# Four experts' results turned by VectorE and carried to rows by transfers, in a fused LSH attention and expert layer

## The chip, the cores and the metric

The kernel runs on one core of one Trainium2 chip. The metric is device time in microseconds (us) of one execution. The core has five engines that matter here: TensorE (PE, with its weight loads shown apart as PEld), VectorE (DVE), ScalarE (ACT), GpSimd (POOL) and SyncE (SP), which here only issues transfers. Each engine takes its own instructions in order and waits for the others by semaphores. SBUF is the core's working memory with 128 partitions, PSUM the memory that TensorE writes.

## The reference

Attention over 4 batches and 8 heads, 768 positions of 64 numbers, where a query sees only the keys in its own hash bucket; then a layer of 8 experts in which each of the 3072 tokens goes to the one expert with the highest gate:

```python
q_bucket = np.sum((np.einsum('bhsd,dk->bhsk', q, proj) > 0) * powers, axis=-1)   # same for k
scores = np.where(q_bucket[..., None] == k_bucket[..., None, :], scale * q @ k.T, -1e9)
x = (softmax(scores) @ v).transpose(0, 2, 1, 3).reshape(3072, 512)
expert_idx = np.argmax(x @ w_gate, axis=1)
gate_w = softmax(x @ w_gate)[np.arange(N), expert_idx]
for e in range(8):                          # tokens sorted by expert
    h = np.maximum(x_sorted[lo:hi] @ w1[e], 0.0)      # 512 -> 1024
    y_sorted[lo:hi] = h @ w2[e]                       # 1024 -> 512
return gate_w[:, None] * y_sorted[inv_perm]
```

The change concerns the expert layer alone.

## The kernel before

**Stages.** The attention part runs first (to about 435 us). Its result rows, with gate and token number behind them, are scattered to a DRAM table `xs`, one region for each expert. Then come the experts in phases `n` of the loop at the end of the kernel function. The experts are ranked by their number of tokens (the first one is picked early). Rank 0 has two phases, n = 0 and 1, of 256 tokens each; n = 2 to 8 are ranks 1 to 7. `PH[n]` holds rank, offset and capacity, from `CAPS`. Tokens beyond a capacity go to a spill loop at the end.

**A phase.** `mm1(n, f)`, f = 0 to 7, makes the 1024 hidden features in eight products of 128 features. Each float32 operand is held as a high and a low part, and three of the four part products are summed, so one result takes 12 matmuls in the first half and 24 in the second. ScalarE writes the ReLU's high part (L827), VectorE the low part (L829). `mm2(n, m)`, m = 0 to 3, makes the output. For the four wide ranks 1 to 4 the output comes feature by token: ScalarE copies it to `YT` (L851), and in the next phase `yout(n - 1, f // 2)` stands behind every second `mm1`: four matmuls with the identity (L876) turn 128 tokens back to rows, VectorE multiplies with the gate (L878), and GpSimd sends the rows to the output by an indirect transfer (L880). For the others (`by_token`) the second product is computed token by feature at once (L867, and in halves at the very end L900).

**Widths.** `products` (L769) runs the first matmul of a group over the whole capacity, and the others over one of four widths in `WIDTHS`, picked by branches from the expert's real length.

**Tokens of the next phase.** `rows(n + 1)`, at a phase's start, loads the next tokens with SP in four transfers (L712) and their gates and numbers in one (L714). `blocks` turns them from SBUF to SBUF by VectorE in 32x32 blocks (L736), and `xt` makes the high part by a ScalarE copy (L755) and the low part by a VectorE subtraction (L756), a quarter of the features at a time. The tables `WHEN` and, for n = 1, `SOON` say behind or within which `mm2` each quarter stands.

**Weights.** They come in chunks, four to an expert: two of w1 and two of w2. SP loads each chunk in halves of 512 KB (`raw_load`, L680) into four buffers; `halves` has ScalarE write the high part (L693) and GpSimd the low part (L694), a quarter of a chunk behind each `mm1` and two behind each `mm2`. Six chunks fit. In SP's order a phase starts with the rows, then the load of the second half of the next expert's second chunk follows (called at f = 1), and its conversion stands at f = 6.

The order of every engine's instructions is the order of the program text.

Of the kernel before, what the change touches and what calls it, by code (L numbers as in the profile page):

```python
# [21 lines left out]
DM = H * D  # L22
# [12 lines left out]
FLOOR = -float(2 ** 33)  # L35
LOW = -float(2 ** 100)

WIDTHS = [(), (456, 440, 432, 416), (432, 424, 408, 392), (408, 400, 388, 372), (396, 384, 376, 360),
          (384, 368, 356, 344), (372, 356, 348, 340), (354, 344, 336, 324)]


EARLY = 256
CAPS = [512, 456, 432, 408, 396, 384, 372, 354]
ROW = N + 128
FILL = 512
NONE = 1 << 20
# [7 lines left out]


@with_exitstack
def lsh_attention_moe(ctx, tc, qk2, v, proj, wg, w1, w1q, w2, out):
    nc = tc.nc
    const = ctx.enter_context(tc.tile_pool(name="const", bufs=1))
    moe = ctx.enter_context(tc.tile_pool(name="moe", bufs=1))  # L60
# [604 lines left out]
    def raw_load(c, a):  # L665

        r, k = divmod(c, 4)
        if k < 2:
            w = w1q if r else w1
            src = w[bass.ds(EV[r], 1)].rearrange("o (a p) f -> p (o a) f", p=128)[:, 2 * a:2 * a + 2,  # L670
                                                                               k * 512:(k + 1) * 512]
        else:
            o = (k - 2) * 4 + 2 * a
            src = w2[bass.ds(EV[r], 1)].rearrange("o (a p) d -> p (o a) d", p=128)[:, o:o + 2, :]
        n = 2 * c + a
        if n < 10 or n % 2:
            t = moe.tile([128, 2, 512], F32, name="raw", bufs=2)
        else:
            t = P2["p"].tile([128, 2, 512], F32, name="raw2", bufs=2)
        nc.sync.dma_start(t, src)  # L680
        RAW[c, a] = t
# [46 lines left out]

        return x[:, d * PW + E:d * PW + E + 2 * D]

    def blocks(n, j):

        if j == 0:
            XT[n] = P2["p"].tile([128, 4, 512], F32, name="xt")
        if j < len(tiles_of(PH[n][2])):
            nc.vector.transpose(XT[n][:, :, 128 * j:128 * j + 128].rearrange("p c (t i) -> p t c i", i=32),  # L736
                                XG[n][:, 4 * j:4 * j + 4].rearrange("p t w -> p (t w)"))

    def xt(n, d):
        r, o, c = PH[n]  # L740
        if d == 0:
            XH[n] = (moe.tile([128, 2, 4, EARLY], F32R, name="xhe") if n < 2 else
                     P2["p"].tile([128, 2, 4, CAPS[1]], F32R, name="xh"))
        t = len(tiles_of(c))
        if n > 1:
            p = XT[n][:, d]
        else:
            p = ps.tile([128, 512], F32, name="t", bufs=2)
            for j in range(t):
                nc.tensor.transpose(p[:, j * 128:(j + 1) * 128], heads(XG[n][:, j], d), ident)  # L750
        if d == 0:
            GT[n] = moe.tile([128, 4], F32, name="gate", bufs=3)
            nc.vector.tensor_copy(GT[n][:, :t], XI[n][:, :t, 0] if n > 1 else XG[n][:, :t, GC])
            tokens(n)
        nc.scalar.activation(XH[n][:, 0, d, :c], p[:, :c], AF.Copy)  # L755
        nc.vector.tensor_tensor(XH[n][:, 1, d, :c], p[:, :c], XH[n][:, 0, d, :c], op=OP.subtract)  # L756
# [72 lines left out]
            nc.vector.scalar_tensor_tensor(h1[:, f, :c], p[:, :c], 0.0, h0[:, f, :c], op0=OP.max, op1=OP.subtract)  # L829

    def by_token(n):
        return PH[n][2] <= 384

    def mm2(n, m, mid=None):

        r, o, c = PH[n]
        if by_token(n):
            yout(n, m, mid)
            return
        if m == 0:  # L840
            YT[n] = (wk.tile([128, 4, EARLY], F32, name="qk") if n == 0 else
                     P2["p"].tile([128, 4, CAPS[1]], F32, name="yt"))
        h = HH[n]
        ms = slice(m * 128, (m + 1) * 128)
        p = ps.tile([128, 512], F32, name="s", bufs=3)
        if mid:
            mid()

        terms = [(CH[4 * r + 2 + f // 4][:, a, f % 4, ms], h[b][:, f]) for f in range(8) for a, b in ((0, 0), (0, 1), (1, 0))]
        products(n, p, c, terms)  # L850
        nc.scalar.activation(YT[n][:, m, :c], p[:, :c], AF.Copy)  # L851

    def yout(n, j, mid=None):
        r, o, c = PH[n]
        if j >= len(tiles_of(c)):
            return
        i, pw = tiles_of(c)[j]
        if n + 1 == len(PH) and j + 1 == len(tiles_of(c)):
            youts(n, j, i, pw)
            return  # L860
        p = ps.tile([128, 512], F32, name="s", bufs=3)
        if by_token(n):
            k = 0
            for f in range(8):
                w = CH[4 * r + 2 + f // 4]
                for a, b in ((0, 0), (1, 0), (0, 1)):
                    nc.tensor.matmul(p[:pw], HH[n][b][:, f, i:i + pw], w[:, a, f % 4],  # L867
                                     start=(k == 0), stop=(k == 23))
                    k += 1
                    if k == (12 if n else 20) and mid:  # L870
                        mid()
        else:

            yw = max(pw, min(128, CAPS[1] - i))
            for m in range(4):
                nc.tensor.transpose(p[:yw, m * 128:(m + 1) * 128], YT[n][:, m, i:i + yw], ident)  # L876
        y = (P2["p"] if n else moe).tile([128, DM], F32, name="y" if n else "ye", bufs=3 if n else 2)
        nc.vector.tensor_scalar(y[:pw], p[:pw], GT[n][:pw, j:j + 1], None, op0=OP.mult)  # L878
        nc.gpsimd.memset(C["spacer"], 0.0)
        st = nc.gpsimd.indirect_dma_start(out=out, out_offset=bass.IndirectOffsetOnAxis(ap=IX[n][:pw, j:j + 1], axis=0),  # L880
                                          in_=y[:pw], in_offset=None, bounds_check=N - 1, oob_is_err=False)
        for q in outs:
            tc.declare_no_dep(st.ins, q.ins, reason="rows of other tokens")
        outs.append(st)

    def youts(n, j, i, pw):

        r = PH[n][0]
        y = P2["p"].tile([128, DM], F32, name="y", bufs=3)
        ix = P2["p"].tile([128, 2], I32, name="ix2")  # L890
        for s in range(2):
            nc.vector.tensor_scalar(ix[:, s:s + 1], IX[n][:, j:j + 1], 2.0, float(s), op0=OP.mult, op1=OP.add)
        for s in range(2):
            cs = slice(s * DM // 2, (s + 1) * DM // 2)
            p = ps.tile([128, 512], F32, name="s", bufs=3)
            k = 0
            for f in range(8):
                w = CH[4 * r + 2 + f // 4]
                for a, b in ((0, 0), (1, 0), (0, 1)):
                    nc.tensor.matmul(p[:pw, :DM // 2], HH[n][b][:, f, i:i + pw], w[:, a, f % 4, cs],  # L900
                                     start=(k == 0), stop=(k == 23))
                    k += 1
            nc.vector.tensor_scalar(y[:pw, cs], p[:pw, :DM // 2], GT[n][:pw, j:j + 1], None, op0=OP.mult)
            st = nc.gpsimd.indirect_dma_start(out=out.rearrange("n (s d) -> (n s) d", s=2),
                                              out_offset=bass.IndirectOffsetOnAxis(ap=ix[:pw, s:s + 1], axis=0),
                                              in_=y[:pw, cs], in_offset=None, bounds_check=2 * N - 1, oob_is_err=False)
            for q in outs:
                tc.declare_no_dep(st.ins, q.ins, reason="other parts of the rows")
            outs.append(st)
# [241 lines left out]


    WHEN = (((), (0,)), ((1,), (2,)), ((3,), ()), ((), ()))
    SOON = (((), ()), ((0, 1), (2, 3)), ((), ()), ((), ()))
    raw_load(5, 0)
    plan = spill_plan()
    for n in range(1, len(PH)):
        c0 = 4 * (PH[n][0] + 1)
        last = n + 1 == len(PH)
        if not last:  # L1160
            rows(n + 1)
            length(n + 1)
        for f in range(8):
            mm1(n, f)
            if f % 2 and not by_token(n - 1):
                yout(n - 1, f // 2)
            halves(c0, f)
            if 3 <= n < 6:
                for _ in range(2):
                    next(plan, None)  # L1170
        for m in range(4):
            mid, end = ((), ()) if last else (WHEN if n > 1 else SOON)[m]
            if m == 0 and not last:
                for j in range(4):
                    blocks(n + 1, j)
            if not (last and m == 3):
                mm2(n, m, lambda: xts(n + 1, mid))
            halves(c0 + 2, 2 * m)
            halves(c0 + 2, 2 * m + 1)
            xts(n + 1, end)  # L1180
        if n == 6:
            for _ in plan:
                pass
        if n == 7:
            C["n"] = nc.values_load(C["cntn"][0:1, 0:1], min_val=0, max_val=TMAX)
# [65 lines left out]
```

## Time and profile before

| | |
|---|---|
| median of 3 runs | 717.42 us (715.97 to 718.87) |
| profiled execution | 715.64 us, span 713.8 us |
| TensorE busy, weight loads busy | 691.8 us, 560.5 us |
| VectorE, ScalarE, GpSimd busy | 491.0, 410.9, 487.6 us |
| DMA, mean over the span | 194 GB/s |
| mean granted TensorE clock | 0.994 of full speed |

The times come from runs without a profile, the rest from one profiled execution. Matmuls are pipelined and their ends are modelled, so a busy TensorE may still be waiting; weight loads are told by their own starts. A page row gives the busy time of a group of instructions, the mean of one, and behind the bar the idle time of the engine before them with what ended it.

### The profile page before, as it was taken

To read this page: it belongs to the slowest core of one execution; us is meant where nothing else is said; L and a number is where in the kernel's file an instruction comes from. 1 tells how busy PE (TensorE), PEld (TensorE's weight loads), DVE (VectorE), ACT (ScalarE), POOL (GpSimd) and SP (SyncE) were. 2 spreads that over 40 slices of the span, in tenths; PEclk is the share of its full clock that TensorE was granted. 3 is DMA by queue.
4 is the path that set the end of the run, shared out by engine and by line. 5 is a ranking of instruction groups with operands and counts; after the bars stand their busy time and mean duration, and the time that the engine had idled before them with its cause. 6 is when DMAs were issued, how large, how long until landed. Compare 5 with 4: busy or idle time off the path is not lost.

```text
span 713.8 us, 13651 instructions
## 1 busy us (share of the span) xinstructions
PE 691.8 (97%) x4539; PEld 560.5 (79%) x4539; DVE 491.0 (69%) x942; ACT 410.9 (58%) x830; POOL 487.6 (68%) x729
## 2 busy tenths in 40 slices
PE   8889999999999999999998999999999999999996
PEld 4677668667766776676666788899999999989895
DVE  7998898889888988898998673424676825232321
ACT  5786678668766876787676633544444444444310
POOL 7766676678777777877785663686666667768522
PEclk8999999999999999999999999999999999999999
DMA  8888779868867677687678247683847474747201
GB/s 324 277 232 234 252 229 289 230 183 233 246 198 213 198 202 226 212 258 185 201 206 234 90 143 217 204 216 120 200 127 199 139 194 139 195 161 202 93 12 40
DMA packets 67775, 138.33 MB, mean 194 GB/s; under 512 B 12883, under 2 KB 29523, under 8 KB 67680
## 3 DMA queue, kind: packets, MB, share of 16 engines
q1 hardware_dynamic: 60848, 120.67, 59.4%
q0 software_dynamic: 6688, 16.35, 6.8%
q8 instruction: 61, 1.00, 0.6%
q14 instruction: 34, 0.28, 0.1%
q10 hardware_dynamic: 144, 0.03, 0.0%
HBM read 75.79 MB, written 26.33 MB: 143 GB/s over the span
## 4 chain that ended last, share of the span: by engine, by line
PE 79%; ACT 10%; issue 6%; DVE 4%; POOL 1%; POOLq 0%; ACTq 0%; DVEq 0%
PE s L769 28%; PE t L411 17%; PE s L867 8%; PE s L309 7%; PE s L311 6%; PE t L349 6%; ACT e L335 5%; DVE m L319 2%; ACT pt L375 2%; PE t L264 2%; PE t L430 2%; ACT bits L277 1%; ACT bits L244 1%; PE s L876 1%; DVE w L389 1%
## 5 line engine op out<-in xcount | busy, mean ns | idle before, releaser
L335 ACT ACTIVATE e<-s,m 128x768 f32<-128x768 f32 x192 | 189.9, 992 | 72.2 <-DVE m L326 36.7
L319 DVE TENSOR_REDUCE m<-s 128x1 f32<-128x768 f32 x192 | 177.6, 946 | 27.9 <-PE s L311 24.0
L694 POOL TENSOR_TENSOR w<-raw,w 128x512 fp32r<-128x512 f32 x112 | 145.2, 1323 | 34.1 <-ACT w L693 33.0
L411 PE MATMUL t<-pt,vt 128*64 128x384 f32 x768 | 130.9, 490 | 1.3 <-ACT e L335 1.3
L769 PE MATMUL s<-xh,w 128*128 128x432 f32 (+11 forms) x672 | 121.9, 338 | 0.0
L769 PEld LDWEIGHTS s<-xh,w 128*128 128x128 f32 x672 | 114.6, 188 | 3.1 <-issue 0.8
L411 PEld LDWEIGHTS t<-pt,vt 128*64 128x64 f32 x768 | 52.5, 137 | 65.1 <-issue 62.5
L829 DVE SCALAR_TENSOR_TENSOR hh<-s,hh 128x256 fp32r<-128x256 f32 (+7 forms) x64 | 35.5, 555 | 95.9 <-ACT hh L827 94.6
L349 PE MATMUL t<-ident,e 128*128 128x128 f32 x612 | 91.0, 276 | 7.8 <-ACT pt L375 4.6
L389 DVE STREAM_TRANSPOSE w<-e 128x768 f32<-128x768 f32 x90 | 84.0, 959 | 9.4 <-ACT e L335 8.6
L349 PEld LDWEIGHTS t<-ident,e 128*128 128x128 f32 x612 | 71.5, 140 | 20.0 <-ACT pt L375 8.3
L827 ACT ACTIVATE hh<-s 128x256 fp32r<-128x256 f32 (+7 forms) x64 | 31.3, 490 | 89.9 <-PE s L769 89.9
L769 PE MATMUL s<-hh,w 128*128 128x432 f32 (+5 forms) x384 | 72.3, 349 | 0.0
L324 POOL TENSOR_SCALAR m<-m 128x1 f32<-128x1 f32 x98 | 22.8, 233 | 70.6 <-DVE m L319 68.4
L693 ACT ACTIVATE w<-raw 128x512 fp32r<-128x512 f32 x112 | 66.7, 623 | 7.4 <-DMA raw<-in_w1q_dram 5.8
L769 PEld LDWEIGHTS s<-hh,w 128*128 128x128 f32 x384 | 69.9, 188 | 1.3
L880 POOL DMA_INDIRECT out_dram<-y,ix x26 | 26.9, 1036 | 58.0 <-DVE y L878 22.9
L375 ACT ACTIVATE pt<-t 128x512 f32<-128x512 f32 (+1 forms) x113 | 63.6, 587 | 3.8 <-PE t L349 3.4
L309 PE MATMUL s<-w 80*128 80x384 f32 x192 | 56.2, 374 | 3.3 <-ACT e L335 2.4
L309 PE MATMUL s<-qk 80*128 80x384 f32 x192 | 57.1, 380 | 1.3 <-ACT e L335 1.0
L867 PE MATMUL s<-w,hh 128*128 128x512 f32 (+1 forms) x240 | 56.4, 394 | 0.0
L867 PEld LDWEIGHTS s<-w,hh 128*128 128x128 f32 (+1 forms) x240 | 44.6, 187 | 10.5
(222 smaller groups left out, 1065.4 us busy)
## 6 DMA issues: line engine op xcount, KB each, us to landing
pt<-w SPq DMA_DIRECT2D x240, 144.0 KB, 3.4
raw<-in_w_dram SPq DMA_DIRECT2D x36, 512.0 KB, 3.9
raw<-in_w1q_dram SPq DMA_DIRECT2D x28, 512.0 KB, 4.9
w<-in_qk_dram SPq DMA_DIRECT2D x14, 768.0 KB, 8.0
xd<-in_qk_dram SPq DMA_DIRECT2D x14, 768.0 KB, 7.3
sorted_rows<-xr SPq DMA_DIRECT2D x8, 1156.0 KB, 12.5
vt<-in_v_dram SPq DMA_DIRECT2D x16, 384.0 KB, 3.0
xg<-sorted_rows SPq DMA_DIRECT2D x16, 256.0 KB, 6.6
```

Source lines behind the costliest of these rows:

```text
L309: nc.tensor.matmul(p[:, a, :HALF], k[0:80, 2, c], k[0:80, 3, n], start=i >= 4, stop=i < 4)
L311: nc.tensor.matmul(p[:, a, :HALF], k[:, 0, c], k[:, 1, n], start=i < 4, stop=i >= 4)
L319: nc.vector.tensor_reduce(m[:, 0:1], p[:, :, :HALF], axis=AX.XY, op=OP.max, negate=True)
L335: nc.scalar.activation(e, p[:, :, :HALF], AF.Exp, bias=m[:, 2:3], scale=m[:, 1:2], accum_out=SM[g, hf][:, t, s:s + 1])
L349: nc.tensor.transpose(p[:, x * 128:(x + 1) * 128], e[w][:, kt // 3, (kt % 3) * 128:(kt % 3) * 128 + 128], ident)
L375: nc.scalar.activation(o, x, AF.Copy)
L389: nc.vector.transpose(d.rearrange("p b k q -> p k b q"), PP.pop(i).rearrange("p a c -> p (a c)"))
L411: nc.tensor.matmul(p[s * 64:(s + 1) * 64, :HALF], VT[g][:, kt, s, :], x, start=(kt == 0), stop=(kt == NT - 1))
L693: nc.scalar.activation(w[:, 0, a], r, AF.Copy)
L694: nc.gpsimd.tensor_tensor(w[:, 1, a], r, w[:, 0, a], op=OP.subtract)
L769: nc.tensor.matmul(p[:, :z], w, x[:, :z], start=first and k == 0, stop=k == len(ts) - 1 and (n < 2 or not first))
L867: nc.tensor.matmul(p[:pw], HH[n][b][:, f, i:i + pw], w[:, a, f % 4], start=(k == 0), stop=(k == 23))
```

## The change

The results of ranks 1 to 4 are no longer turned by TensorE. The columns of their w2 are reordered on the host (`w2q`), so that each `mm2` gives 32 features of each of four groups; VectorE turns the result in 32x32 blocks out of PSUM into `YT`; `carry`, at the start of the next phase, moves the blocks to rows in `YR` with 16 SP transfers of 32 partitions and up to 2 KB in a piece; `back` multiplies with the gates on ScalarE and sends the rows. `back` stands behind f = 6 and 7 of the next phase and behind its first two `mm2`. The next tokens are turned straight into PSUM, a quarter at a time within `xt`, and `blocks` goes; `SOON` lies one step earlier. Capacities and widths of ranks 1 to 4 become multiples of 32. The output buffer `y` has two copies in place of three.

```diff
-WIDTHS = [(), (456, 440, 432, 416), (432, 424, 408, 392), (408, 400, 388, 372), (396, 384, 376, 360),
+WIDTHS = [(), (448, 440, 432, 416), (448, 424, 408, 392), (416, 400, 388, 372), (384, 376, 364, 352),
-CAPS = [512, 456, 432, 408, 396, 384, 372, 354]
+CAPS = [512, 448, 448, 416, 384, 384, 372, 354]
+WIDE = 5
 def raw_load(c, a):
-            src = w2[bass.ds(EV[r], 1)].rearrange("o (a p) d -> p (o a) d", p=128)[:, o:o + 2, :]
+            w = w2q if 0 < r < WIDE else w2
+            src = w[bass.ds(EV[r], 1)].rearrange("o (a p) d -> p (o a) d", p=128)[:, o:o + 2, :]
 def xt(n, d):
+        p = ps.tile([128, 512], F32, name="t", bufs=2)
         if n > 1:
-            p = XT[n][:, d]
+            b = (c + 31) // 32
+            nc.vector.transpose(p[:, :32 * b].rearrange("p (t i) -> p t i", i=32), XG[n][:, :b, 32 * d:32 * d + 32])
 def by_token(n):
-        return PH[n][2] <= 384
+        return not 0 < PH[n][0] < WIDE
 def mm2(n, m, mid=None):
-        nc.scalar.activation(YT[n][:, m, :c], p[:, :c], AF.Copy)
+        y = YT[n][:, :, :, 32 * m:32 * m + 32]
+        g, b = divmod(c // 32, 4)
+        nc.vector.transpose(y[:, :, :g].rearrange("p b j i -> p j b i"), p[:, :128 * g].rearrange("p (j b i) -> p j b i", b=4, i=32))
+        if b:
+            nc.vector.transpose(y[:, :b, g], p[:, 128 * g:c].rearrange("p (b i) -> p b i", i=32))
+    def carry(n):
+        y = YR[n] = P2["p"].tile([128, 4, 4, 2 * D], F32, name="yr")
+        for b in range(4):
+            g = len(range(b, PH[n][2] // 32, 4))
+            for a in range(4):
+                nc.sync.dma_start(y[32 * b:32 * b + 32, a, :g], YT[n][32 * a:32 * a + 32, b, :g])
+    def back(n, j):
+        if j >= len(tiles_of(PH[n][2])):
+            return
+        pw = tiles_of(PH[n][2])[j][1]
+        y = P2["p"].tile([128, DM], F32, name="y", bufs=2)
+        nc.scalar.activation(y[:pw].rearrange("p (a f) -> p a f", a=4), YR[n][:pw, :, j], AF.Copy, scale=GT[n][:pw, j:j + 1])
+        send(n, j, y, pw)
-    SOON = (((), ()), ((0, 1), (2, 3)), ((), ()), ((), ()))
+    SOON = (((0,), (1,)), ((2,), (3,)), ((), ()), ((), ()))
     for n in range(1, len(PH)):
+        if not by_token(n - 1):
+            carry(n - 1)
         if not last:
             rows(n + 1)
             length(n + 1)
         for f in range(8):
             mm1(n, f)
-            if f % 2 and not by_token(n - 1):
-                yout(n - 1, f // 2)
+            if f > 5 and not by_token(n - 1):
+                back(n - 1, f - 6)
             halves(c0, f)
         for m in range(4):
-            if m == 0 and not last:
-                for j in range(4):
-                    blocks(n + 1, j)
             if not (last and m == 3):
                 mm2(n, m, lambda: xts(n + 1, mid))
+            if m < 2 and not by_token(n - 1):
+                back(n - 1, m + 2)
             halves(c0 + 2, 2 * m)
```

`send` holds the two GpSimd instructions that `yout` had (the `spacer` write and the indirect transfer).

## Rows read from the trace of the kernel before

**Rows 1.** Page, busy time in us, share of the span, instructions.
```profile
PE 691.8 (97%) x4539; PEld 560.5 (79%) x4539; DVE 491.0 (69%) x942; ACT 410.9 (58%) x830; POOL 487.6 (68%) x729
```

**Rows 2.** Timeline of weight loads, expert phases: start, length, instructions [idle before].
```profile
460.70 1.41 PEld L769 LDWEIGHTS s<-xh,w 128*128 128x128 f32 x7
...
480.18 18.91 PEld L769 LDWEIGHTS s<-hh,w 128*128 128x128 f32 x96
499.09 4.72 PEld L769 LDWEIGHTS s<-xh,w 128*128 128x128 f32 x24
...
519.75 18.39 PEld L769 LDWEIGHTS s<-hh,w 128*128 128x128 f32 x96
538.15 4.39 PEld L769 LDWEIGHTS s<-xh,w 128*128 128x128 f32 x24
...
557.84 17.46 PEld L769 LDWEIGHTS s<-hh,w 128*128 128x128 f32 x96
575.29 4.15 PEld L769 LDWEIGHTS s<-xh,w 128*128 128x128 f32 x24
...
593.60 16.47 PEld L769 LDWEIGHTS s<-hh,w 128*128 128x128 f32 x96
610.05 3.86 PEld L769 LDWEIGHTS s<-xh,w 128*128 128x128 f32 x24
...
627.09 16.51 PEld L867 LDWEIGHTS s<-w,hh 128*128 128x128 f32 x72
643.64 15.25 PEld L769 LDWEIGHTS s<-xh,w 128*128 128x128 f32 x96
```

**Rows 3.** Groups by shape, 440 to 714 us: busy, mean ns | idle before.
```profile
L769 PE MATMUL s<-xh,w 128*128 128x376 f32 x88 | 16.3, 333 | 0.0
L769 PE MATMUL s<-xh,w 128*128 128x344 f32 x88 | 15.1, 319 | 0.0
L769 PE MATMUL s<-xh,w 128*128 128x340 f32 x88 | 15.1, 319 | 0.0
```

**Rows 4.** SP issues by line (ns min/median/max), and SP's timeline (start, length).
```profile
L400 SPq DMA_DIRECT2D pt<-w x240: 507/590/1926, 35.5 to 386.2; - x120
...
DMA to landing us min/median/max: 2.4/3.4/6.0
...
301.33 7.99 SPq L400 DMA_DIRECT2D pt<-w  x12
...
L712 SPq DMA_DIRECT2D xg<-sorted_rows x28: 321/337/1702, 438.6 to 651.0; - x28
...
538.20 3.30 SPq L712 DMA_DIRECT2D xg<-sorted_rows  x4
...
542.97 1.00 SPq L680 DMA_DIRECT2D raw<-in_w1q_dram  x1
...
575.53 2.25 SPq L712 DMA_DIRECT2D xg<-sorted_rows  x4
...
580.01 0.38 SPq L680 DMA_DIRECT2D raw<-in_w1q_dram  x1
```

**Rows 5.** Page, DMA issues: KB each, us from issue to landing.
```profile
raw<-in_w1q_dram SPq DMA_DIRECT2D x28, 512.0 KB, 4.9
```

**Rows 6.** Groups: busy us, mean ns | idle before, releaser.
```profile
L736 DVE STREAM_TRANSPOSE xt<-xg 128x512 f32<-128x512 f32 x25 | 15.6, 676 | 0.0
...
L829 DVE SCALAR_TENSOR_TENSOR hh<-s,hh 128x256 fp32r<-128x256 f32 (+7 forms) x64 | 35.5, 555 | 95.9 <-ACT hh L827 94.6
...
L827 ACT ACTIVATE hh<-s 128x256 fp32r<-128x256 f32 (+7 forms) x64 | 31.3, 490 | 89.9 <-PE s L769 89.9
...
L693 ACT ACTIVATE w<-raw 128x512 fp32r<-128x512 f32 x112 | 66.7, 623 | 7.4 <-DMA raw<-in_w1q_dram 5.8
```

**Rows 7.** VectorE's timeline at the end of phase 1.
```profile
461.13 0.75 DVE L878 TENSOR_SCALAR y<-s,gate 128x512 f32<-128x512 f32 x1 [3.58 <-PE s L867]
461.80 1.17 DVE L756 TENSOR_TENSOR xh<-xt,xh 128x456 fp32r<-128x456 f32 x2
```

More of the change, by code (lines that the diff above doesn't have):

```diff
@@ L56, in lsh_attention_moe @@
 @with_exitstack
-def lsh_attention_moe(ctx, tc, qk2, v, proj, wg, w1, w1q, w2, out):
+def lsh_attention_moe(ctx, tc, qk2, v, proj, wg, w1, w1q, w2, w2q, out):
     nc = tc.nc
@@ L729, in heads @@
         return x[:, d * PW + E:d * PW + E + 2 * D]
[L731 to L737, printed above, removed]
     def xt(n, d):
@@ L744, in xt @@
         t = len(tiles_of(c))
+        p = ps.tile([128, 512], F32, name="t", bufs=2)
         if n > 1:
-            p = XT[n][:, d]
+            b = (c + 31) // 32
+            nc.vector.transpose(p[:, :32 * b].rearrange("p (t i) -> p t i", i=32), XG[n][:, :b, 32 * d:32 * d + 32])
         else:
-            p = ps.tile([128, 512], F32, name="t", bufs=2)
             for j in range(t):
@@ L840, in mm2 @@
         if m == 0:
-            YT[n] = (wk.tile([128, 4, EARLY], F32, name="qk") if n == 0 else
-                     P2["p"].tile([128, 4, CAPS[1]], F32, name="yt"))
+            YT[n] = P2["p"].tile([128, 4, 4, 2 * D], F32, name="yt")
         h = HH[n]
@@ L850, in mm2, with send @@
         products(n, p, c, terms)
-        nc.scalar.activation(YT[n][:, m, :c], p[:, :c], AF.Copy)
+        y = YT[n][:, :, :, 32 * m:32 * m + 32]
[3 more added lines that the diff above has]
+            nc.vector.transpose(y[:, :b, g], p[:, 128 * g:c].rearrange("p (b i) -> p b i", i=32))
+    YR = {}
+    def carry(n):
[11 more added lines that the diff above has]
+        send(n, j, y, pw)
+    def send(n, j, y, pw):
+        nc.gpsimd.memset(C["spacer"], 0.0)
+        st = nc.gpsimd.indirect_dma_start(out=out, out_offset=bass.IndirectOffsetOnAxis(ap=IX[n][:pw, j:j + 1], axis=0),
+                                          in_=y[:pw], in_offset=None, bounds_check=N - 1, oob_is_err=False)
+        for q in outs:
+            tc.declare_no_dep(st.ins, q.ins, reason="rows of other tokens")
+        outs.append(st)
     def yout(n, j, mid=None):
@@ L861, in yout @@
         p = ps.tile([128, 512], F32, name="s", bufs=3)
[L862 to L877, printed above, removed]
-        nc.vector.tensor_scalar(y[:pw], p[:pw], GT[n][:pw, j:j + 1], None, op0=OP.mult)
[L879 to L884, printed above, removed]
+        k = 0
+        for f in range(8):
+            w = CH[4 * r + 2 + f // 4]
+            for a, b in ((0, 0), (1, 0), (0, 1)):
+                nc.tensor.matmul(p[:pw], HH[n][b][:, f, i:i + pw], w[:, a, f % 4],
+                                 start=(k == 0), stop=(k == 23))
+                k += 1
+                if k == (12 if n else 20) and mid:
+                    mid()
+        y = (P2["p"] if n else moe).tile([128, DM], F32, name="y" if n else "ye", bufs=2)
+        nc.vector.tensor_scalar(y[:pw], p[:pw], GT[n][:pw, j:j + 1], None, op0=OP.mult)
+        send(n, j, y, pw)
     def youts(n, j, i, pw):
         r = PH[n][0]
-        y = P2["p"].tile([128, DM], F32, name="y", bufs=3)
+        y = P2["p"].tile([128, DM], F32, name="y", bufs=2)
         ix = P2["p"].tile([128, 2], I32, name="ix2")
@@ L1242 @@
               "in_w1_dram": np.ascontiguousarray(inputs["moe_w1"]),
-              "in_w1q_dram": np.ascontiguousarray(inputs["moe_w1"].reshape(E, 4, 4, 32, F).transpose(0, 2, 1, 3, 4)).reshape(E, DM, F), "in_w2_dram": np.ascontiguousarray(inputs["moe_w2"])}
+              "in_w1q_dram": np.ascontiguousarray(inputs["moe_w1"].reshape(E, 4, 4, 32, F).transpose(0, 2, 1, 3, 4)).reshape(E, DM, F), "in_w2_dram": np.ascontiguousarray(inputs["moe_w2"]),
+              "in_w2q_dram": np.ascontiguousarray(inputs["moe_w2"].reshape(E, F, 4, 4, 32).transpose(0, 1, 3, 2, 4)).reshape(E, F, DM)}
     nc = bacc.Bacc("TRN2", target_bir_lowering=False, num_devices=1, dynamic_dma_scratch_size=2048)
```

## The prediction

> **What bounds the kernel now.** I read the page's busy table first: TensorE (PE) is busy for 691.8 of 713.8 us [rows 1]. A modelled busy share does not tell waiting from working, so the second view was TensorE's weight loads in order of time over the expert phases [rows 2]. There is one load for each product, and a gap between them is a true stop. The reader is to see that the stretches follow each other almost without a gap: 96 loads take 18.39 us in phase 3's second half (519.75), then 538.15 begins at once. Phases are counted by the loop's n; phases 2 to 5 are ranks 1 to 4, whose results are turned. The third view, the costliest groups, says what the others do meanwhile: ScalarE's ReLU (L827) idles 89.9 us on TensorE, and VectorE's subtraction (L829) 95.9 us on that ReLU [rows 6]. So from phase 2 on an instruction taken off TensorE is worth its full time, and one added to VectorE or ScalarE costs nothing until TensorE waits for it. The fourth view was SP's queue, since the change puts 64 transfers there [rows 4].
>
> **Transposes leave TensorE.** Each wide expert has 16 (L876), four after every second product of the next phase's first half: 64 in all, in phases 3 to 6. I cost them by whole halves, which includes the switching. Phase 3's first half runs from 499.09 to 519.75, 20.66 us, and holds 96 products. The second half has 96 products of the same width without transposes: 18.40 us by its start and the next start, 538.15. Difference 2.26. Phase 4: 538.15 to 557.84 is 19.69, against 17.45 to 575.29: 2.24. Phase 5: 18.31 against 16.45: 1.86. Phase 6 has its second half in another form, so I take phase 7's first half, 15.25 us at 340 columns, as 15.43 at phase 6's 344: 17.04 less 15.43 is 1.61 [rows 2, 3]. The sum is 7.97 us, or 0.50 for each group of four. Some of it is stops that stand beside the transposes and may stay. I take 7.5, with 7.0 and 8.0 as ends.
>
> **Widths and capacities.** They change only what the first product of each group covers. The other products run at the width picked from the expert's length: 376 columns in phase 5, for instance [rows 3], and 376 is in the new list as well. So are 432, 424 and 400, the widths picked for ranks 1 to 3 in the same view. The first products move by -8, +16, +8 and -12 columns, 12 of each: under 0.1 us net. Rank 4 now has three token tiles in place of four, which removes work only from the turned path.
>
> **VectorE and ScalarE.** The turn of SBUF into SBUF (L736, 0.676 us) becomes four turns into PSUM for each phase; four results per wide expert are turned out of PSUM by one or two instructions; the gate's four multiplications go from VectorE to ScalarE, which loses four copies. No row shows a turn that reads or writes PSUM. The nearest is L736, and from the other side L829, which reads PSUM, at 0.555 [rows 6]. At 0.5 to 1.4 us for each result both ends are far below the 4.1 us (16.45 / 4) and more that 24 products take, and three PSUM buffers stand behind. Cost nothing; the cover is TensorE's own time, and if it were gone every excess would be paid once for each of 16 results.
>
> **Phase 2's start.** The order SOON moves one step forward: the last quarter of the tokens is now turned after the gate multiplication of phase 1's second result, where before only its subtraction was left. That multiplication starts at 461.13 and takes 0.75; two subtractions followed from 461.80 in 1.17, so to 462.97 [rows 7]. The loads show what TensorE lost there: phase 2's first half, 460.70 to 480.18, is 19.48 us, its second half 18.91 [rows 2], a difference of 0.57. Now a turn (0.65), a ScalarE copy (0.57, estimated from the ReLU's 0.49 at narrower tiles) and a subtraction (0.6, from L829's 0.555 in the same way [rows 6]) follow 461.88, to 463.8 with the handovers. That is 0.8 later, of which I count 0.7, because the first product of a group needs the last quarter only at its tenth term. Ends: 0 (if the copy is earlier) and 1.0.
>
> **The carry on SP.** This is where I had to choose. Each of phases 3 to 6 now starts, on SP, with 16 transfers of 32 pieces of up to 2 KB. They wait for VectorE's last turn, about 1.2 us after the phase's first load (estimated as one result's eviction). Queued behind them are the next phase's rows and one load of weights (the second half of chunk 4r+5), whose conversion by ScalarE stands ahead of the eighth ReLU of the phase. TensorE needs that ReLU's low half in the 23rd product of the next result. So the chain is, from a phase's first load: 1.2 + 16p + (rows, until the weight load issues) + 4.9 landing [rows 5] + 0.62 conversion (L693) + 0.49 ReLU + 0.56 subtraction [rows 6]. In phase 5 the rows take from 575.53 to 580.01, 4.48 us [rows 4], so the low half is ready 12.3 + 16p after the phase's start. Without transposes TensorE asks for it at 16.45 + 22 x 0.171 = 20.2. Slack for 16p: 7.9 us. Phase 4 (538.20 to 542.97, 4.77 us [rows 4]; 17.45 + 22 x 0.182): 8.9. Phases 3 and 6, worked the same way with rows of 4.5 and 3.6 us, have 10.3 and about 9.2.
> What does p cost? The nearest row is the exchange of the attention part: SBUF to SBUF, 32 partitions, 144 KB for 64 KB here. One issue is 0.507 at the least, 0.590 median; twelve in a row took 7.99 us, or 0.67 each [rows 4]. From below: a weight load's issue with its registers fits within 0.42, since an issue of the rows, also with registers, is 0.337 at the median [rows 4]. From above: four transfers of rows in 3.30 us, 0.83 each under load [rows 4]. Fewer bytes should keep the queue from filling, so I take the least of the nearest row and a gap of 0.06: 0.57, that is 9.1 us for 16. Stall: 1.2 in phase 5, 0.2 in phase 4, none in 3 and 6: 1.4 us. At 0.50 or less it is nothing; at 0.67 (10.7 us) it is 0.4 + 1.8 + 2.8 + 1.5 = 6.5.
> The data themselves are in time: 1.2 + 9.1 + 3.4 landing [rows 4] is 13.7 us after a phase's start, and ScalarE asks for them after its seventh ReLU, seven eighths into a first half, at 13.5 to 16.
> The exchange's row shows 0.67 us an issue at 32 pieces and 144 KB, and no row has fewer bytes in as many pieces [rows 4]. The Trainium skill, "DMA: Bandwidth & Descriptors", section Bandwidth, says that transfers under 64 KB are descriptor-dominated: the cost would go with the pieces and not fall with the bytes. By that p would stay near 0.67 and the change would be worth about 0.3 us instead of 5.4. The rows' own issues speak against counting pieces alone: 0.337 at the median, at 512 pieces each [rows 4].
>
> **Sum.** -7.5 + 0.7 + 1.4 = -5.4 us. The profiled execution took 715.64 us, its span 713.8 and 1.8 around it; the median of the runs shown is 717.42, 1.8 above that. 715.64 - 5.4 = 710.2, and with the 1.8 to the median: 712.0.
>
> **Rivals.** (B) The carry issues fast, p at most 0.50, and TensorE's small stops go too: -8.0 + 0 to 0.7, so 709.4 to 710.1. For it: the bytes are less than half. Against: 0.507 was the least of 240 exchange issues. (C) The gain is given back on SP: p near 0.67, the weights late by 6.5 us in all, -7.5 + 0.7 + 6.5 = -0.3: 717.1. For it: that is the nearest row's pace. Against: that pace held at over twice the bytes. (D) The other side: the same place at the price that the rows show under load, 0.83 (13.2 us). Stalls 2.9 + 4.3 + 5.3 + 4.0 = 16.5, so 717.4 - 6.8 + 16.5 = 727. It decides from p = 0.67 upward. For it: the carry starts when rows and weights also move. Against: the loaded price was seen on transfers of 512 pieces. (E) The change doesn't do what it says: turning out of PSUM takes longer than a result's products and becomes the bound. It would need over 4.1 us where the nearest rows have 0.6 to 0.7; at 5 us each, against 4.4 on the average of the four phases, it would be 16 x 0.6, about +10 less 6.8: 720.6.
>
> **Chances.** Forecast 0.50, B 0.19, C 0.17, D 0.11, E 0.03. A measurement of this kernel can tell about 0.5%, 3.6 us, from no change: faster means under 713.8. The forecast's own range is 710 to 714.5, and about 0.42 of its 0.50 lies under 713.8; with B that is faster 0.61. Same: 0.08 and C with a little of D, 0.25. Slower: 0.14. The range goes from B's 709 to 718.5, which leaves out most of D and E and a little of B's far side.
>
> **What would show it.** Right: no product with the identity among TensorE's work after phase 2; first halves of phases 3 to 6 near 18.4, 17.5, 16.5 and 15.4 us; SP's 16 transfers in about 9 us from each phase's start; at most a gap of about a microsecond in the weight loads near the end of phase 5's first result, with ScalarE waiting for a weight load before it. Wrong: SP's 16 transfers over 10.5 us and gaps in three or four phases (C, D); VectorE's turns over 2 us (E); a first half of phase 2 under 19.3 or over 21 us (SOON mis-sized); TensorE waiting for anything else in phases 3 to 6, a place that I have not priced.

## The result and the profile after

The changed kernel takes 722.34 us (median of 7 runs, 720.78 to 727.1); the kernel before took 718.05 in the same comparison. The ratio is 1.008, interval 1.0052 to 1.0108: slower, where -5.4 us was forecast, and outside the range of 709 to 718.5. The profiled execution took 722.25 us, its span 720.4, 6.6 us above the span before.

The weight loads over the expert phases, which answer to [rows 2], tell where the time went (start, length, instructions, and the gap before them with its releaser):

```profile
462.38 1.79 PEld L764 LDWEIGHTS s<-xh,w 128*128 128x128 f32 x9
464.75 0.19 PEld L764 LDWEIGHTS s<-xh,w 128*128 128x128 f32 x1 [0.58 <-ACT xh L750]
...
482.54 18.82 PEld L764 LDWEIGHTS s<-hh,w 128*128 128x128 f32 x96
501.36 18.48 PEld L764 LDWEIGHTS s<-xh,w 128*128 128x128 f32 x96
519.85 4.06 PEld L764 LDWEIGHTS s<-hh,w 128*128 128x128 f32 x21
524.94 0.19 PEld L764 LDWEIGHTS s<-hh,w 128*128 128x128 f32 x1 [1.03 <-ACT hh L822]
525.59 0.49 PEld L764 LDWEIGHTS s<-hh,w 128*128 128x128 f32 x3 [0.47 <-DVE hh L824]
...
539.83 17.47 PEld L764 LDWEIGHTS s<-xh,w 128*128 128x128 f32 x96
557.28 3.81 PEld L764 LDWEIGHTS s<-hh,w 128*128 128x128 f32 x21
562.69 0.19 PEld L764 LDWEIGHTS s<-hh,w 128*128 128x128 f32 x1 [1.60 <-ACT hh L822]
...
576.71 16.65 PEld L764 LDWEIGHTS s<-xh,w 128*128 128x128 f32 x96
593.34 3.65 PEld L764 LDWEIGHTS s<-hh,w 128*128 128x128 f32 x21
599.87 0.26 PEld L764 LDWEIGHTS s<-hh,w 128*128 128x128 f32 x1 [2.88 <-ACT hh L822]
600.46 14.06 PEld L764 LDWEIGHTS s<-hh,w 128*128 128x128 f32 x74 [0.33 <-DVE hh L824]
614.50 15.33 PEld L764 LDWEIGHTS s<-xh,w 128*128 128x128 f32 x96
629.80 4.70 PEld L892 LDWEIGHTS s<-w,hh 128*128 128x128 f32 x21
637.20 0.30 PEld L892 LDWEIGHTS s<-w,hh 128*128 128x128 f32 x2 [2.71 <-ACT hh L822]
637.80 12.44 PEld L892 LDWEIGHTS s<-w,hh 128*128 128x128 f32 x49 [0.29 <-DVE hh L824]
650.28 15.14 PEld L764 LDWEIGHTS s<-xh,w 128*128 128x128 f32 x96
```

The first halves of phases 3 to 6 are free of transposes and fell from 20.66, 19.69, 18.31 and 17.04 us [rows 2] to 18.49, 17.45, 16.63 and 15.30: 7.8 us gained. The second halves rose from 18.40, 17.45, 16.45 and 16.55 to 19.98, 19.43, 21.16 and 20.48: 12.2 us lost. Every one of them stops after 21 products, before the 22nd, which needs the eighth ReLU's high part, and again one or two products later for the low part. The gaps, with the small ones that the lines above leave out, are 1.66, 2.21, 3.21 and 3.00 us, 10.1 in all. The other 2.1 lie in phases 5 and 6 (1.5 and 0.9, against -0.1 and -0.2 in phases 3 and 4), where the clock was lower, as shown below. Phase 2's first half took 20.16 against 19.48. So phases 3 to 6 cost 4.4 us and phase 2 costs 0.7. Of the span's 6.6 us another 1.9 stand before the first expert phase, which began at 440.07 in place of 438.20 (left open below), and the rest of the kernel gave about 0.3 back.

SP's queue in phase 5, with the 16 transfers of phases 3, 4 and 6 around it, answers to [rows 4] (start, length, count):

```profile
502.50 10.93 SPq L859 DMA_DIRECT2D yr<-yt  x16
...
540.96 11.68 SPq L859 DMA_DIRECT2D yr<-yt  x16
...
577.79 11.47 SPq L859 DMA_DIRECT2D yr<-yt  x16
589.48 1.99 SPq L714 DMA_DIRECT2D xg<-sorted_rows  x4
591.65 0.39 SPq L716 DMA_DIRECT2D xi<-sorted_rows  x1
592.14 0.42 SPq L656 DMA_DIRECT2D spill_rows<-tab  x1
592.83 0.38 SPq L682 DMA_DIRECT2D raw<-in_w1q_dram  x1
...
615.49 11.78 SPq L859 DMA_DIRECT2D yr<-yt  x16
```

ScalarE at the same place:

```profile
591.63 0.49 ACT L822 ACTIVATE hh<-s 128x384 fp32r<-128x384 f32 x1 [1.07 <-PE s L764]
592.02 0.71 ACT L867 ACTIVATE y<-yr,gate 128x512 f32<-128x512 f32 x1
598.81 0.63 ACT L695 ACTIVATE w<-raw 128x512 fp32r<-128x512 f32 x1 [6.08 <-DMA raw<-in_w1q_dram]
599.35 0.47 ACT L822 ACTIVATE hh<-s 128x384 fp32r<-128x384 f32 x1
```

Read the two together. The 16 transfers hold SP for 11.47 us from 1.1 us after the phase's start, so the weight load issues at 592.83, 16.1 us into the phase (4.7 before the change). ScalarE has done the seventh ReLU at 592.1, multiplies the carried rows without waiting, then waits 6.08 us for that load. The eighth ReLU, whose sum TensorE had ready at 593.5, comes at 599.35, and TensorE goes on at 599.87.

The windows around the gaps of phases 3, 5 and 6 (length, then busy time of PE, PEld, DVE, ACT and POOL with instructions, granted clock as a share of full speed, DMA share, GB/s):

```profile
525.00:530.00 5.00, 4.80 (x23) 4.27 (x24) 4.35 (x10) 3.18 (x6) 4.52 (x7) 1.00 0.78 273
...
595.00:600.00 5.00, 2.44 (x15) 2.12 (x13) 0.15 (x1) 1.19 (x3) 0.47 (x1) 0.99 0.96 334
600.00:605.00 5.00, 5.00 (x20) 4.67 (x21) 3.36 (x8) 3.63 (x8) 4.56 (x7) 0.67 0.59 195
605.00:610.00 5.00, 5.00 (x31) 5.00 (x30) 2.86 (x6) 2.81 (x6) 4.81 (x6) 1.00 0.70 240
...
635.00:640.00 5.00, 2.80 (x7) 2.12 (x8) 1.89 (x4) 2.13 (x4) 2.96 (x4) 0.75 0.88 327
```

After the gap of 2.88 us the granted clock is 0.67 over five microseconds, so part of them ran at the lower of the two levels (1.2 and 2.4 GHz), and TensorE started 20 products there instead of 30 or 31. The gap of 2.71 us in phase 6 is followed by 0.75 and then 0.91; after the gaps of phases 3 and 4 the windows show 1.00.

### The profile page after: what moved, and what is told of

The parts are those of the page before. It is cut to its first block, busy times and chain, and to the rows that moved or that the text cites. A ratio compares the mean times of both kernels' runs of the same rounds, so it can differ in the third digit from the quotient of the medians.

```text
span 720.4 us, 13630 instructions
## 1 busy us (share of the span) xinstructions
PE 691.2 (96%) x4475; PEld 558.5 (78%) x4475; DVE 478.1 (66%) x957; ACT 413.0 (57%) x829; POOL 482.9 (67%) x727
## 4 chain that ended last, share of the span: by engine, by line
PE 69%; ACT 9%; issue 7%; DVE 5%; SPq 4%; DMA 3%; POOL 2%; POOLq 0%; another core or an unknown queue 0%; ACTq 0%; DVEq 0%
PE s L764 19%; PE t L412 17%; PE s L310 8%; PE s L892 7%; PE s L312 7%; PE t L350 7%; ACT e L336 5%; DMA raw<-in_w1q_dram 3%; SPq L859 3%; DVE m L320 2%; PE t L431 2%; PE t L265 2%; POOL w L696 2%; ACT pt L376 1%; ACT bits L245 1%
## 5 line engine op out<-in xcount | busy, mean ns | idle before, releaser
L696 POOL TENSOR_TENSOR w<-raw,w 128x512 fp32r<-128x512 f32 x112 | 142.7, 1297 | 63.2 <-ACT w L695 62.3
L764 PE MATMUL s<-xh,w 128*128 128x432 f32 (+11 forms) x672 | 118.5, 336 | 0.5 <-ACT xh L750 0.2
L824 DVE SCALAR_TENSOR_TENSOR hh<-s,hh 128x448 fp32r<-128x448 f32 (+5 forms) x64 | 35.6, 556 | 103.7 <-ACT hh L822 102.0
L764 PE MATMUL s<-hh,w 128*128 128x400 f32 (+5 forms) x384 | 75.2, 355 | 4.9 <-ACT hh L822 4.5
L822 ACT ACTIVATE hh<-s 128x448 fp32r<-128x448 f32 (+5 forms) x64 | 31.2, 488 | 78.3 <-PE s L764 78.3
L892 PEld LDWEIGHTS s<-w,hh 128*128 128x128 f32 (+1 forms) x240 | 45.6, 191 | 12.8 <-ACT hh L822 2.7
L312 PE MATMUL s<-qk 128*128 128x384 f32 x192 | 51.2, 348 | 0.5 <-DVE qk L230 0.5
```

Source lines behind the costliest of these rows:

```text
L312: nc.tensor.matmul(p[:, a, :HALF], k[:, 0, c], k[:, 1, n], start=i < 4, stop=i >= 4)
L696: nc.gpsimd.tensor_tensor(w[:, 1, a], r, w[:, 0, a], op=OP.subtract)
L764: nc.tensor.matmul(p[:, :z], w, x[:, :z], start=first and k == 0, stop=k == len(ts) - 1 and (n < 2 or not first))
```

## The experiments

Each ratio is to runs of the kernel before made beside it, with medians of 717.14 (e1 to e4), 717.01 (e5 to e8) and 716.12 us (e9 to e11). Theory SP, the one that the texts below test: the transfers' issue time holds back the weight load, and ScalarE's order turns that into TensorE's gap. Rivals: the bytes carried (DATA), or VectorE's turning (TURN).

### e1_relu_first

```diff
-            halves(c0, f)
+            if f == 7:
+                halves(c0, 6)
+            if f != 6:
+                halves(c0, f)
```

> The changed kernel with one edit: ScalarE's conversion of the seventh quarter of weights (behind f = 6) is moved behind the eighth ReLU. SP's queue, its 16 transfers and the late weight load stay as they are. Theory SP: TensorE lost its time because that conversion waited for the late load and the eighth ReLU stood behind it in ScalarE's order. Then the gaps of phases 3 to 6 (1.7, 2.2, 3.2 and 3.0 us in the trace of the changed kernel) and the low clock after them (some 2.6 us) go although the weights come as late as before: 722.3 - 12 = 710 to 711.5, about 1% under the kernel before. Rival DATA: the late weights or the transfers' traffic hold TensorE itself: no more than 3 us better, 719 or above. Rival TURN: VectorE's turning out of and into PSUM costs the time: no change, 722.

713.46 us, ratio 0.9954 (0.9939 to 0.997). The gaps of phases 3 to 6 are gone: their second halves take 18.58, 17.31, 16.64 and 16.30 us. The transfers, the late load and the turns are as in the changed kernel, so one place in ScalarE's order is enough to end these gaps, which settles TURN and DATA for them. But the gain is 3.7 us and not the 5.6 to 7 expected; 4.3 us of gaps stand at the start of phase 7 instead:

```profile
638.20 1.05 PEld L764 LDWEIGHTS s<-xh,w 128*128 128x128 f32 x6
642.40 0.19 PEld L764 LDWEIGHTS s<-xh,w 128*128 128x128 f32 x1 [3.15 <-ACT xh L750]
```

ScalarE and VectorE in phase 6 of the same kernel show what made the tokens of phase 7 late: the load, which comes no earlier than before, and a wait for a free `y`, behind which the turn and the copy of the last tokens follow at once:

```profile
632.48 1.15 ACT L695 ACTIVATE w<-raw 128x512 fp32r<-128x512 f32 x2 [7.03 <-DMA raw<-in_w1q_dram]
...
640.59 0.75 DVE L898 TENSOR_SCALAR y<-s,gate 128x512 f32<-128x512 f32 x1 [2.40 <-DMA out_dram<-y,ix]
641.25 0.58 DVE L742 STREAM_TRANSPOSE t<-xg 128x384 f32<-128x384 f32 x1
...
641.87 0.48 ACT L750 ACTIVATE xh<-t 128x372 fp32r<-128x372 f32 x1 [3.22 <-DVE t L742]
```

### e2_carry_behind

```diff
-        if not by_token(n - 1):
-            carry(n - 1)
...
-            if f > 5 and not by_token(n - 1):
-                back(n - 1, f - 6)
+            if f == 7 and not by_token(n - 1):
+                back(n - 1, 0)
             halves(c0, f)
+            if f == 1 and not by_token(n - 1):
+                carry(n - 1)
...
-            if m < 2 and not by_token(n - 1):
-                back(n - 1, m + 2)
+            if m < 3 and not by_token(n - 1):
+                back(n - 1, m + 1)
```

> The changed kernel with the 16 transfers put on SP behind the next rows and the weight load (after f = 1), and the four multiplications of the carried rows one step later each (behind f = 7 and the first three results). Nothing else. Theory SP: the weight load issues within 5 us of a phase's start as before the change, ScalarE's conversion does not wait, no gap: 710 to 711.5. The transfers then land near 19 us after a phase's start, and ScalarE's wait for them stands behind the eighth ReLU, where TensorE needs nothing from it. Rival DATA: the same bytes move in the same phase, so the loss stays to half or more: 717 or above. Rival TURN: 722.

716.94 us, ratio 0.9995 (0.9979 to 1.0011): missed. Phases 3 to 6 have no gap, as the theory has it, but phase 7 starts with 5.1 us of them. ScalarE in phase 6:

```profile
631.38 0.72 ACT L867 ACTIVATE y<-yr,gate 128x512 f32<-128x512 f32 x1 [7.83 <-DMA yr<-yt]
...
637.89 0.72 ACT L867 ACTIVATE y<-yr,gate 128x512 f32<-128x512 f32 x1 [5.26 <-DMA out_dram<-y,ix]
```

Two waits stand ahead of the next tokens' copies: for the carried rows, which now land 24 us into the phase, and for a copy of `y`. I had said that TensorE needs nothing from ScalarE there; it needs the next phase's tokens.

### e8_carry_behind_y3

e2 with the third copy of `y` back, here and at the two other places where `y` is made:

```diff
-        y = P2["p"].tile([128, DM], F32, name="y", bufs=2)
+        y = P2["p"].tile([128, DM], F32, name="y", bufs=3)
```

> e2 with three copies of y in place of two, nothing else. If e2's gap at phase 7's start comes from ScalarE and VectorE waiting for a free y (5.3 us of waiting for the output transfer in e2's trace), it goes: 711 to 713. If it comes from ScalarE's wait for the carried rows (7.8 us in e2's phase 6), it stays: 715 to 717.

712.14 us, ratio 0.9933 (0.9904 to 0.9963), and no gap at phase 7's start, where 85 loads follow each other from 638.68. So in e2 it was the wait for `y` that decided.

### e10_y3_only

The changed kernel with the same edit and nothing else.

> The changed kernel with three copies of y in place of two, nothing else: SP's 16 transfers stand at the front as before. Theory SP: the gaps of phases 3 to 6 come from the late weight load, which y does not touch: 721 to 723. If y's two copies were a part of the loss (they ended e2's phase 6), 719 or below.

722.73 us, ratio 1.009 (1.0055 to 1.0125). The gaps of phases 3 to 6 are there as before, up to 4.11 us, and 12.8 in all in its profiled execution, the slowest of its five (727.99); the copies of `y` are no part of this change's loss that the time shows. In e1 and e2 they count, where the gaps of phases 3 to 6 are gone.

### e3_24_issues

```diff
-                nc.sync.dma_start(y[32 * b:32 * b + 32, a, :g], YT[n][32 * a:32 * a + 32, b, :g])
+                for j in ((slice(0, 2), slice(2, g)) if b < 2 else (slice(0, g),)):
+                    nc.sync.dma_start(y[32 * b:32 * b + 32, a, j], YT[n][32 * a:32 * a + 32, b, j])
```

> The changed kernel with the same bytes carried in 24 transfers a phase instead of 16 (the eight that have four blocks in a piece, or three, are cut in two). Theory SP, by the price of an issue: 8 more issues of 0.65 to 0.73 us hold the weight load 5.2 to 5.8 us longer in each of four phases, and each microsecond ends in TensorE's gap: +21 to 23 us and a few more of low clock, 743 to 750. Theory by bytes (the issue pace follows the data): the 24 take as long as the 16, no change, 722 to 724.

749.35 us, ratio 1.0441 (1.0412 to 1.047). SP's timeline in phases 3 and 5:

```profile
501.76 16.31 SPq L860 DMA_DIRECT2D yr<-yt  x24
...
592.57 18.67 SPq L860 DMA_DIRECT2D yr<-yt  x24
```

The four phases take 0.68 to 0.78 us an issue, against 0.68 to 0.74 for 16 transfers of the same bytes in all: time goes with the number of transfers and not with their bytes. The pieces grow with the transfers here, 32 to each, so e3 alone cannot tell one from the other. The gaps grew to 7.0, 7.7, 10.7 and 8.9 us. DATA falls.

### e7_two_queues

`carry` now takes the queue and the list of transfers to issue:

```diff
-            carry(n - 1)
+            carry(n - 1, nc.sync, [(b, a) for b in range(4) for a in range(2)])
...
             mm1(n, f)
+            if f < 4 and not by_token(n - 1):
+                carry(n - 1, nc.scalar, [(f, 2), (f, 3)])
```

> The changed kernel with 8 of the 16 transfers issued from ScalarE's queue, two behind each of the first four ReLUs; the other 8 stay on SP at the phase's start, ahead of rows and weights. Same bytes, same pieces, y with two copies. Theory SP: SP is held 5.7 us instead of 11.4, the weight load lands near 16 us after a phase's start, ScalarE's conversion waits little, the gaps of phases 3 to 6 (10.1 us) go or shrink to under 1 us, and with them the low clock: 710 to 713. Rival DATA (bytes, not issues): 720 or above. Against ScalarE: 8 issues of 0.6 us are 4.8 us a phase, beside 20 us of idle time; if they delay ReLUs, gaps appear in the first half of each phase, 714 to 718.

709.17 us, ratio 0.9898 (0.9874 to 0.9922): 7.8 us under the kernel before and 13 under the changed one, with the same bytes in the same pieces. Its weight loads have no gap from phase 3 to 6; SP in phase 5 is done with its share in 5.57 us:

```profile
573.06 16.65 PEld L764 LDWEIGHTS s<-xh,w 128*128 128x128 f32 x96
589.70 16.66 PEld L764 LDWEIGHTS s<-hh,w 128*128 128x128 f32 x96
606.34 15.33 PEld L764 LDWEIGHTS s<-xh,w 128*128 128x128 f32 x96
```

```profile
574.15 5.57 SPq L861 DMA_DIRECT2D yr<-yt  x8
579.93 3.25 SPq L714 DMA_DIRECT2D xg<-sorted_rows  x4
...
584.71 0.38 SPq L682 DMA_DIRECT2D raw<-in_w1q_dram  x1
```

The weight load issues 11.7 us into the phase instead of 16.1, and that is early enough. ScalarE's own 8 issues cost TensorE nothing.

### e11_12_on_sp

Against e7:

```diff
-            carry(n - 1, nc.sync, [(b, a) for b in range(4) for a in range(2)])
+            carry(n - 1, nc.sync, [(b, a) for b in range(4) for a in range(3)])
...
-                carry(n - 1, nc.scalar, [(f, 2), (f, 3)])
+                carry(n - 1, nc.scalar, [(f, 3)])
```

> e7 with 12 transfers on SP and 4 on ScalarE's queue (one behind each of the first four ReLUs). Theory SP as a threshold: the weight load issues 4 x 0.71 = 2.8 us earlier than in the changed kernel, and each gap shrinks by that: 1.7, 2.2, 3.2 and 3.0 us become 0, 0, 0.4 and 0.2, and the low clock after them goes as well: 709 to 712, near e7 and not halfway (716) between e7 and the changed kernel. A loss in proportion to the issues on SP would give 715 to 717.

712.38 us, ratio 0.9937 (0.9911 to 0.9962), just above the expected 712. Phases 3 and 4 have no gap, phases 5 and 6 have 1.69 and 0.47:

```profile
595.40 0.19 PEld L764 LDWEIGHTS s<-hh,w 128*128 128x128 f32 x1 [1.10 <-ACT hh L822]
...
629.03 0.30 PEld L894 LDWEIGHTS s<-w,hh 128*128 128x128 f32 x2 [0.17 <-ACT hh L822]
```

With 8, 12, 16 and 24 transfers on SP ahead of the load, the gaps of phases 3 to 6 are 0, 2.2, 10.1 and about 34 us: a slack that is used up first, then about a microsecond of TensorE for a microsecond of SP (from 16 to 24 transfers SP is held 23 us longer and the gaps grow by 24). Phase 5 has the largest gap and phase 3 the smallest of the changed kernel, as their slacks in the prediction have it; phases 4 and 6 stand the other way round.

### e4_tokens_only

The kernel before with the token part alone (`blocks` gone, `xt` turning into PSUM, the new `SOON`).

> The kernel before with the token part alone: the next tokens turned straight into PSUM a quarter at a time, the turns from SBUF to SBUF gone, SOON one step earlier. Results are turned by TensorE as before, no carry. Theory SP: this part costs only phase 2's start, +0.6 us, so 718 to 719.5, and the gaps of phases 3 to 6 are absent. Rival TURN: turning into PSUM is part of the loss, 720 or above. If it saves VectorE or GpSimd time that counts, 716 or below.

717.03 us, ratio 1.0003 (0.999 to 1.0015), below the 718 to 719.5 expected. Phase 2's first half takes 20.20 us in place of 19.48, so the 0.7 is there in the trace, too little to show in the time. Turning into PSUM costs nothing else that shows.

### e5_backs_last and e6_soon

e5 is e8 with all `back` at the end of the phase, one behind the third result and three behind the fourth; e6 is e5 with this:

```diff
-    SOON = (((0,), (1,)), ((2,), (3,)), ((), ()), ((), ()))
+    SOON = (((0,), (1,)), ((2, 3), ()), ((), ()), ((), ()))
```

> The 16 transfers stand on SP behind the rows and the weight load (as in e2), all four multiplications of the carried rows stand at the end of the phase (one behind the third result, three behind the fourth), and y has three copies again as before the change. Theory SP with ORDER: nothing that TensorE needs in a phase stands behind a wait for the carried rows any more, so phases 3 to 6 run as in e2 without a gap and phase 7 starts without its gap too: 717.1 - 7.8 (transposes) + 0.6 (phase 2's start) = 710, within 709 to 711.5. Rival CLOCK: e2's missing gain was a lower clock at the start of the run and not the gap at phase 7: 713 or above.

> e5 with phase 2's third and fourth quarters of tokens both turned within phase 1's second result, ahead of its gate multiplication. Theory: the last quarter no longer waits for that multiplication, phase 2 starts without the 1.2 us of gaps of the changed kernel: 0.8 to 1.2 us under e5, 709 to 710. If the gaps come from the turn itself and not from its place, the same as e5.

722.47 us, ratio 1.0077 (1.0046 to 1.0107), and 721.75, 1.0078 (1.0052 to 1.0104): both missed, and on the wrong side. The last of the phase's multiplications waits for a copy of `y`, now ahead of the next phase's first ReLUs (ScalarE, then the weight load it held, at the start of phase 6 in e5):

```profile
618.86 0.72 ACT L867 ACTIVATE y<-yr,gate 32x512 f32<-32x512 f32 x1 [4.66 <-DMA out_dram<-y,ix]
619.49 0.46 ACT L822 ACTIVATE hh<-s 128x384 fp32r<-128x384 f32 x1
```

```profile
620.59 0.19 PEld L764 LDWEIGHTS s<-xh,w 128*128 128x128 f32 x1 [1.65 <-DVE hh L824]
```

My theory of the place was incomplete: in an engine's order some later instruction is always needed, here across the phase's border. e6 did show its own point: phase 2's first half is 18.87 us without a gap, against 20.23 in e5.

### e9_two_queues_soon_y3

e7 with e6's `SOON` and the third `y`.

> e7 (8 transfers from SP, 8 from ScalarE's queue) with phase 2's last two quarters of tokens turned ahead of phase 1's last gate multiplication (as in e6) and three copies of y. Theory: phase 2's first half falls from 20.2 to 18.9 us as it did in e6, the rest stays as in e7: 709.2 - 1.3 = 707.5 to 708.5. If y's copies still cost something in e7, up to 1 us more. If nothing of it counts, 709.

709.03 us, ratio 0.9892 (0.9861 to 0.9922), where 707.5 to 708.5 was expected. Its first half of phase 2 is 18.88 us, but the time cannot be told from e7's. The two are the best versions, about 1% under the kernel before.

## Why the prediction was wrong

- **Transposes leave TensorE, -7.5 us:** right, 7.8 in the first halves. In e7 all of it is left: its first halves are as short, and its second halves take 68.8 us together, as before the change.
- **Phase 2's start, +0.7:** right (0.68 in the changed kernel, 0.72 in e4), by the step given: the last quarter behind the gate multiplication.
- **Widths, VectorE, ScalarE at nothing:** right. The loads run at the old pace (the second halves of e7), e4 shows no cost of the turn into PSUM, and a result's turn out of PSUM took 0.58 us and at most 0.21 for the rest, far under the time of its products. The capacities, the first width of each rank, became multiples of 32, but not all the narrower widths did (440 and 376 are none); the text ahead of the prediction says it of all.
- **The carry on SP, the price p of an issue: this is the term that failed.** The forecast took 0.57 us and 9.1 for 16. Measured were 10.93, 11.68, 11.47 and 11.78 us in the four phases, 0.68 to 0.74 each. I argued that fewer bytes keep the queue from filling; e3 shows that the price does not fall with the bytes. The nearest row had stood at 0.67 [rows 4], and I took its least with a small gap and not its pace in a row. The excess, 1.8, 2.6, 2.4 and 2.7 us, is most of the gaps: taken off, 1.66, 2.21, 3.21 and 3.00 become 0, 0, 0.8 and 0.3, near the 1.4 us of the forecast. The other way round, the four measured times against the prediction's own slacks (10.3, 8.9, 7.9 and 9.2) give 9.6 us of gaps, where 10.1 were measured. The mechanism was the forecast's; this term's size was not.
- **The rest of the chain:** its links were right. The transfers started 1.0 to 1.1 us into a phase (1.2 forecast), the carried data were in time, ScalarE waited for the load and TensorE for the eighth ReLU. Two sizes were off and nearly cancel: the load took 6.0 us to conversion in phase 5 and not 4.9, and the rows held SP 3.35 and not 4.48.
- **What was not priced at all:** the clock. The gaps of 2.88 and 2.71 us were followed by a granted clock of 0.67 and 0.75 over five microseconds. The 2.1 us of the second halves that are not gaps are put down to it, as a difference; no experiment parts them from the gaps.
- **The rivals:** the kernel landed between C (717.1) and D (727), on their mechanism and at the price that lies between theirs. All four phases had gaps and the 16 transfers took over 10.5 us, the sign named for C and D. The point that D named, 0.67, decided: at it the prediction's own sum is about no change, and 0.05 us more for each issue, with the clock, made the kernel slower. The break-even was about 0.1 us above my price, in a term that counts 64 times, and 28% for C and D together was little for that.
- The rule in the Trainium skill, "DMA: Bandwidth & Descriptors", section Bandwidth (transfers under 64 KB are descriptor-dominated), stands there beside times of whole transfers, loads that GpSimd issues, and not beside times of an issue. Carried over to the issue, as the prediction did, it would have put p near 0.67, closer to the 0.68 to 0.74 measured. e3, with smaller transfers at the same price, agrees that bytes do not set it; transfers of 512 pieces that issue in 0.34 [rows 4] speak against pieces alone, though they read from DRAM.
- The same page of the Trainium skill, section Issuing engines are not separate DMA queues, says that issuing from several engines only saves the sequencers' issue time. e7 agrees that it saves that time (SP held for 5.57 us in place of 11.47 in phase 5), and here this was worth 13 us, because a weight load stood behind it.

What stays open: in most profiled executions of the kernels with the carry, the expert phases begin 1.3 to 2.9 us later than in that of the kernel before (phase 1 at 439.5 to 441.1 against 438.2 us), though the program text of the attention part is the same; e6's begins at 438.8 and e5's at 436.5. The granted clock of the stretch from 10 to 20 us varies from 0.50 to 1.00 among these executions. Whether the change shifts that, or chance does, was not tried.

## What to carry to other kernels

Before work is moved from a full engine to transfers, count the transfers and not the bytes, multiply by the issue time that the nearest transfers show when many stand in a row (0.67 here, and even that was a little low), and look at what is next in that queue: here one weight load behind 16 small transfers cost more than the 64 transposes saved. Follow the late one to the instruction that stands behind it in the next engine's order. Splitting the issues over two queues returned everything; moving the waits to another place in the same order returned some of it or none.

## What the runs showed of the hardware that was not expected

- A transfer between SBUF partitions held SP for 0.68 to 0.74 us in a row of 16 (48 and 64 KB each, changed kernel) and for 0.68 to 0.78 in a row of 24 (16 to 48 KB, e3), about what 144 KB took before (0.67); the issue itself was 0.59 at the median. ScalarE's queue took 0.60 at the median for the same transfers in e7. The number is not all: rows of 8 took 0.63 to 0.75 (e7), and rows of 16 right behind a weight load 0.75 to 0.88 (e2, e5, e6, e8). What sets the pace within this range is not shown.
- In the changed kernel gaps of 1.03 and 1.60 us in TensorE's work left its granted clock at 1.00, and one of 2.88 us was followed by five microseconds at a mean of 0.67. The length of one gap does not tell it: in e5 one of 1.65 us (620.59, another of 0.55 behind it) was followed by 0.55 from 623 to 626, and one of 1.67 (655.90, 0.35 behind it) by 1.00.
